# Parked blocks of the last weight matrix: stored split, loaded once, two quarters converted later

## The chip, the cores and the metric

The kernel runs on one core of a Trainium2 chip. The metric is the device time of one execution in microseconds (us), as the median of several runs. A core has a matrix engine (TensorE, PE in the profile, with its weight loads as PEld), a vector engine (VectorE, DVE), a scalar engine (ScalarE, ACT), GpSimd (POOL) and SyncE (SP). Here POOL and SP mostly issue DMA transfers. Each engine executes its own list of instructions in order; semaphores tie the lists to each other and to the transfers.

## The reference

Four stages follow each other over 2304 tokens (4 batches of 576) with 512 features:

```python
def phi(x):
    proj = einsum('bhsd,df->bhsf', x, w_phi)
    proj = proj - max(abs(proj), axis=-1, keepdims=True)
    return concatenate([exp(proj), exp(-proj)], axis=-1)
q_p, k_p = phi(q), phi(k)
kv = einsum('bhsf,bhsd->bhfd', k_p, v);  z = sum(k_p, axis=2)
x = einsum('bhsf,bhfd->bhsd', q_p, kv) / (einsum('bhsf,bhf->bhs', q_p, z) + 1e-6)
x = maximum(maximum(x @ w1, x @ w2), x @ w3) @ w_out      # 512 -> 768 -> 512
h = x @ w_in                                              # 512 -> 2048
out = (maximum(h, 0) + alpha * minimum(h, 0)) @ w_out2    # 2048 -> 512
```

Weights arrive as 64-bit floats, the rest as 32-bit floats.

## The kernel before, in words

**Arithmetic.** A float product is made of three PE products: each operand is split into a high part (`fp32r`, a rounded copy made on ACT at L70) and a low part (the difference, made on DVE at L76). `three()` lists high x high, high x low and low x high. A 64-bit weight is first converted by `from_f64` into a 32-bit word: one step on ACT (L83), four on DVE (L85, L87, L89, L91).

**Stages.** Linear attention fills the first part, interleaved with layer 1. Layer 1 (`layer1`, L427) makes three products in three PSUM banks `p1`, then the maximum: ACT copies the first (`s1`, L441), DVE takes the maximum with the second (L442) and the third (`ho`, L444), POOL stores it to h_d (L446). From about 324 us on only layer 1 is left (the tail, loop at L616); beside its products the weights of later layers are converted, `convert(2)` after each unit. Layer 2 (loop at L653, PE at L664) multiplies by w_out for eight chunks of 288 tokens, and stores sums and differences of the results (`yo`, `yt`) to y_d. Layer 3 (loop at L788, PE at L757) computes x @ w_in by seven products for each of 16 units (4 token tiles x 4 quarters of the features): `sums` in one double bank, copied by ACT as `s` (L766), with `pb` and `pc` in others; PReLU follows (L776, L777) and POOL stores `g` to g_d (L778). Layer 4 (loop at L823, PE at L841) makes the output in nine blocks of 256 tokens, two halves each; a half has seven factors `o` (`left`, L695: loads `a` from g_d, four sums or differences on DVE at L718 to L731, then seven splits) times seven blocks of the last weight matrix (`wq`), 84 matmuls a half.

**The last weight matrix.** It comes in four quarters p. For each, `do_quarters(p)` (L532) loads four pieces of 512 KB into "st" buffers (`big`, L499; three of them), converts them into words in "wt" buffers (`word`, L502; eight), and makes seven combined blocks with three differences and three more words (L517). `park` (L529) stores each block of 256 KB to q_d in DRAM; POOL issues the store (L530). The blocks are needed in layer 4 only, and until then no SBUF is free for them. `split_q` (L737), called in the last token tile of layer 3 and at the start of layer 4, fetches the 28 blocks: SP loads a word (L742), and ACT and DVE split it into a `wq` granule of 512 KB, in a slot (`ring`, `ring2`) that PE has released.

**Order.** `todo` is the list of conversion steps: quarters 0 to 3, w_out, then w_in (`do_quad`). `convert(n)` takes n steps from it and is called at fixed places. The framework's scheduler then sets the order of the instructions on each engine, by priorities and its own model of durations; the built program keeps that order. A buffer that is reused makes its next writer wait until all uses of the former content are done, the landing of a store included.

Of the kernel before, what the change touches and what calls it, by code (L numbers as in the profile page):

```python
# [10 lines left out]
F32 = mybir.dt.float32  # L11
F32R = mybir.dt.float32r
# [7 lines left out]
P = 128  # L20
# [33 lines left out]
def tile_kernel(ctx: ExitStack, tc: tile.TileContext, qT, kT, tails, v, w_phi, w1, w2, w3, w_out, w_in, w_out2, alpha, out):  # L54
# [11 lines left out]
    nc = tc.nc  # L66
# [36 lines left out]
    ring = ctx.enter_context(tc.tile_pool(name="ring", bufs=18, side="left"))  # L103
    dram = ctx.enter_context(tc.tile_pool(name="dram", bufs=1, space=DRAM))
# [4 lines left out]
    r_d = dram.tile([B, NPAIR, 2, S], F32, name="r_d")  # L109
    g_d = dram.tile([NF2, P, NTOK], F32, name="g_d")  # L110
    y_d = dram.tile([NT2, 7, P, 2 * CH], F32, name="y_d")
    q_d = dram.tile([4, 7, P, 512], F32, name="q_d")

    def bank(tag, bufs, nm):
        return ps.tile([P, 512], F32, tag=tag, bufs=bufs, name=nm)
# [342 lines left out]
    for i, pair in enumerate(pairs):  # L458
# [9 lines left out]
        for j in range(count):  # L468
            for _ in range(min(count, 4) if j == 0 else int(j + 3 < count)):
                fetch(begun[pair])  # L470
            with tc.high_priority(offset=LAST if i < NPAIR - 1 else 0):
                n = sum(len(x) for x in w)
                run(split_w123(n // 3, n % 3))
        u0 = 3 * (i - NPAIR) - LAG
        for u in range(u0, u0 + 3):
            if u >= 0:
                c, f = (u % 2, u // 2) if u < 12 else (u // NF1 % 2, u % NF1)
# [8 lines left out]
    def granule(pool, nm):  # L486

        return pool.tile([P, 2, 512], F32R, tag="w", name=nm)
# [8 lines left out]
            staged.append(st)  # L497

    def big(dtype, shape, nm):  # L499
        return sp.tile(shape, dtype, tag="st", bufs=3, name=nm)  # L500

    def word():  # L502
        return sp.tile([P, 512], F32, tag="wt", bufs=8, name="wt")
# [8 lines left out]
    def split(dst, src):  # L512
        hi_act(dst[:, 0], src)
        sub(V, dst[:, 1], src, dst[:, 0])
# [5 lines left out]
    wo, wi, wq = {}, {}, {}  # L520
# [5 lines left out]
    def do_out():  # L526
        return [lambda k=k: split_out(k) for k in range(NF1)], [w_out[k] for k in range(NF1)]

    def park(p, i, x):  # L529
        nc.gpsimd.dma_start(q_d[p, i], x)  # L530

    def do_quarters(p):  # L532
        b = {}

        def get(q):
            b[q] = words()

        def one():
            get(0)
            b[4] = both(word(), b[1], b[0])  # L540
            park(p, 0, b[0])
            park(p, 4, b[4])

        def two():
            get(3)
            park(p, 2, b[3])
            b[5] = both(word(), b[3], b[4])
            park(p, 5, b[5])
            park(p, 6, both(b[1], b[3], b[1]))

        def three_():
            get(2)
            park(p, 1, b[2])
            park(p, 3, both(word(), b[5], b[2]))

        return [lambda: get(1), one, two, three_], [w_out2[p, q] for q in (1, 0, 3, 2)]

    def do_quad(q):
        x = {}
        wi[q] = {}  # L560

        def get(n):
            x[n] = words()

        def to(i, n):
            pool = ring2 if (q == 0 and i < 4) or (q == 3 and i > 0) else ring
            wi[q][i] = granule(pool, "wi")
            split(wi[q][i], x[n])

        def second():  # L570
            get("22")
            x["s1"] = both(word(), x["21"], x["22"], ALU.add)

        def third():
            get("11")
            x["s2"] = both(word(), x["s1"], x["11"])
            x["s3"] = both(x["21"], x["11"], x["21"])
            to(0, "11")

        def fourth():  # L580
            get("12")
            to(1, "12")
            x["s4"] = both(x["12"], x["12"], x["s2"])

        steps = [lambda: get("21"), second, third, fourth]
        steps += [lambda i=i, n=n: to(i, n) for i, n in zip(range(2, 7), ("s2", "s1", "s3", "22", "s4"))]
        return steps, [w_in[q, a, b] for a, b in ((1, 0), (1, 1), (0, 0), (0, 1))]

    for steps, src in [do_quarters(p) for p in range(4)] + [do_out()] + [do_quad(q) for q in range(4)]:
        todo += steps  # L590
        sources += src

# [19 lines left out]
    def convert(n):  # L612
        for _ in range(min(n, len(todo))):
            todo.pop(0)()
# [38 lines left out]
    for c in range(2 * B):  # L653
        p2 = [double(tag, "p2") for tag in SETS[c % 2]]
        if c == 0:
            p2.reverse()
        if c + 1 < 2 * B:
            for kk in range(NF1 // 2):
                load_h(c + 1, kk)
        for ms in ((0, 1), (2, 3)) if c == 0 else (range(KT),):  # L660
            for k, m in ((k, m) for k in range(NF1) for m in ms):
                cs = slice(m * P, (m + 1) * P)
                for n, (x, y) in enumerate(three(wo[k][:, 0, cs], wo[k][:, 1, cs], *hs[c, k])):
                    nc.tensor.matmul(p2[m // 2][1][:, m % 2], x, y, start=k + n == 0, stop=k == NF1 - 1 and n == 2)  # L664
        tp = c // 2
        for b in range(2):
            Y[b, c % 2] = yo = z_tile("yo")
            A.activation(yo, p2[b][1], AF.Copy)
            if c % 2 == 0:
                nc.scalar.dma_start(y_d[tp, b], flat(yo))  # L670
        if c % 2:
            nc.scalar.dma_start(y_d[tp, 6], flat(Y[1, 1]))
            t1, t2, t3 = (z_tile("yt") for _ in range(3))
            both(t1, Y[0, 1], Y[0, 0])
            both(t2, Y[1, 1], t1)
            both(t3, Y[1, 1], Y[0, 1])
            t4 = both(Y[1, 0], Y[1, 0], t2)
            for i, t in zip((2, 3, 4, 5), (t2, t1, t3, t4)):
                nc.gpsimd.dma_start(y_d[tp, i], flat(t))
        if c == 2 * B - 1:  # L680
            for i in range(6):
                load_y(0, i)
        convert(3)

    T = P
    ORDER = (0, 5, 6, 4, 1, 3, 2)
# [50 lines left out]
    def split_q(count):  # L737
        for _ in range(count):
            n = len(wq)
            p, i = needs[n]  # L740
            wl = word()
            nc.sync.dma_start(wl, q_d[p, i])  # L742
            wq[p, i] = granule(ring if n < 16 or n >= 26 else ring2, "wq")
            split(wq[p, i], wl)

    load_y(0, 6)

# [40 lines left out]
    for n, (tp, q) in enumerate(units):  # L788
        sums, u1 = nxt
        if (tp, q) == (NT2 - 1, 0):  # L790
            convert(len(todo))
        g0, g1 = result(), result()
        _, pb = double("db", "pb")
        mults(pb, tp, q, 1, True)
        V.tensor_tensor(g0[:, :, 0], pb, u1, op=ALU.add)
        mults(sums, tp, q, 2, False)
        u2 = kept(sums)
        _, pc = double("dc", "pc")
        mults(pc, tp, q, 3, True)
        mults(sums, tp, q, 4, False)  # L800
        u3 = kept(sums)
        V.tensor_tensor(g1[:, :, 1], pc, u3, op=ALU.add)
        if n + 1 < len(units):
            nxt = begin(n + 1)
        mults(sums, tp, q, 5, False)
        A.activation(g1[:, :, 0], sums, AF.Copy)
        mults(pc, tp, q, 6, False)
        V.tensor_tensor(g0[:, :, 1], pc, u2, op=ALU.add)  # L808
        prelu(g1, tp, 4 * q + 2)
        prelu(g0, tp, 4 * q)  # L810
        convert(3)
        if tp == NT2 - 1:
            if q == 0:
                first = left(0, 0)
                run(first)
            split_q((2, 7, 7, 7)[q])
# [105 lines left out]
```

## Time and profile before

| | |
|---|---|
| median of 3 runs | 883.93 us (883.5 to 884.14) |
| profiled execution, its own time | 882.21 us |
| its span, first to last instruction | 880.4 us |
| PE busy | 869.1 us, 99% of the span |
| DVE, ACT, POOL busy | 678.7, 490.8, 158.3 us |
| bytes moved by DMA | 142.99 MB, mean 162 GB/s |
| mean granted TensorE clock | 0.998 of full speed |

The page of the profile gives busy times of the engines, the span in 40 slices, the DMA queues, the chain of work that ended last, and the groups of instructions with the idle time before them and what ended it. The trace behind it is read by views: the waits of an engine, the timeline of a window, busy times and DMA rates by window, and the time from issue to landing of transfers.

### The profile page before, as it was taken

To read this page: it belongs to the slowest core of one execution; us is meant where nothing else is said; L and a number is where in the kernel's file an instruction comes from. 1 tells how busy PE (TensorE), PEld (TensorE's weight loads), DVE (VectorE), ACT (ScalarE), POOL (GpSimd) and SP (SyncE) were. 2 spreads that over 40 slices of the span, in tenths; PEclk is the share of its full clock that TensorE was granted. 3 is DMA by queue.
4 is the path that set the end of the run, shared out by engine and by line. 5 is a ranking of instruction groups with operands and counts; after the bars stand their busy time and mean duration, and the time that the engine had idled before them with its cause. 6 is when DMAs were issued, how large, how long until landed. Compare 5 with 4: busy or idle time off the path is not lost.

```text
span 880.4 us, 17440 instructions
## 1 busy us (share of the span) xinstructions
PE 869.1 (99%) x6631; PEld 856.2 (97%) x6631; DVE 678.7 (77%) x1290; ACT 490.8 (56%) x1017; POOL 158.3 (18%) x278
## 2 busy tenths in 40 slices
PE   9999999999999999999999999999999999999998
PEld 8888999999999999999999999999999999999998
DVE  5689878778887879889999454746488889977791
ACT  4677657677776752334365354646477654444440
POOL 0354213222232135331101001111111100000000
PEclk9999999999999999999999999999999999999999
DMA  6455553222332158886489644835358645544321
GB/s 233 140 159 168 169 180 91 77 79 89 85 90 76 29 176 286 291 276 191 159 284 304 203 147 146 271 131 194 111 183 267 214 152 173 165 123 140 120 73 48
DMA packets 70436, 142.99 MB, mean 162 GB/s; under 512 B 9152, under 2 KB 36176, under 8 KB 70352
## 3 DMA queue, kind: packets, MB, share of 16 engines
q1 hardware_dynamic: 53664, 92.95, 33.8%
q0 software_dynamic: 14816, 45.26, 15.0%
q10 hardware_dynamic: 1872, 3.67, 1.2%
q8 instruction: 52, 0.85, 0.4%
q14 instruction: 32, 0.26, 0.1%
HBM read 93.07 MB, written 46.34 MB: 158 GB/s over the span
## 4 chain that ended last, share of the span: by engine, by line
PE 85%; DVE 6%; DMA 4%; issue 2%; ACT 1%; POOL 1%; DVEq 0%; POOLq 0%; ACTq 0%; SPq 0%
PE acc L841 20%; PE p L270 17%; PE sums L757 11%; PE p L664 8%; PE pj L270 6%; PE pn L270 6%; PE pc L757 6%; PE kvp L298 3%; PE kvp L311 3%; PE pb L757 3%; PE pt L373 2%; DVE wt L89 1%; DVE wt L91 1%; DMA xr<-h_d 1%; DMA nd<-nd 1%
## 5 line engine op out<-in xcount | busy, mean ns | idle before, releaser
L270 PE MATMUL p<-x,w123t 128*128 128x288 f32 x1728 | 249.1, 298 | 0.9 <-DVE ho L444 0.9
L270 PEld LDWEIGHTS p<-x,w123t 128*128 128x128 f32 x1728 | 234.5, 188 | 2.2 <-DVE ho L444 1.1
L841 PE MATMUL acc<-wq,o 128*128 128x256 f32 x1512 | 182.3, 283 | 2.5 <-ACT o L70 2.2
L841 PEld LDWEIGHTS acc<-wq,o 128*128 128x128 f32 x1512 | 181.5, 190 | 2.9 <-ACT o L70 2.4
L757 PE MATMUL sums<-x,wi 128*128 128x288 f32 x768 | 107.7, 295 | 0.3 <-ACT s L766 0.3
L757 PEld LDWEIGHTS sums<-x,wi 128*128 128x128 f32 x768 | 103.9, 188 | 0.6 <-ACT s L766 0.6
L664 PE MATMUL p<-x,wo 128*128 128x288 f32 x576 | 77.1, 296 | 1.5 <-ACT x L70 0.8
L664 PEld LDWEIGHTS p<-x,wo 128*128 128x128 f32 x576 | 76.6, 188 | 1.9 <-ACT x L70 1.0
L70 ACT ACTIVATE o<-wt 128x512 fp32r<-128x512 f32 x72 | 44.4, 629 | 56.4 <-PE acc L841 28.6
L777 DVE SCALAR_TENSOR_TENSOR g<-neg,al,g 128x576 f32<-128x576 f32 x64 | 50.1, 811 | 23.7 <-ACT neg L776 23.7
L217 DVE TENSOR_REDUCE mx<-pj 128x4 f32<-128x512 f32 (+1 forms) x80 | 49.7, 629 | 18.4 <-PE pj L270 18.1
L766 ACT ACTIVATE s<-sums 128x576 f32<-128x576 f32 x48 | 31.1, 648 | 45.4 <-PE sums L757 44.1
L778 POOL DMA_DIRECT2D g_d<-g x32 | 22.9, 714 | 162.5 <-DVE g L777 160.2
L446 POOL DMA_DIRECT2D h_d<-ho x48 | 27.8, 579 | 120.5 <-DVE ho L444 102.6
L76 DVE TENSOR_TENSOR o<-wt,o 128x512 fp32r<-128x512 f32 x72 | 48.0, 681 | 1.7 <-ACT o L70 1.7
L83 ACT ACTIVATE wt<-st 128x512 f32<-128x512 f32 x38 | 25.3, 673 | 41.7 <-DMA st<-in_w_out 33.4
L250 ACT ACTIVATE ke<-pj,mx 128x128 f32<-128x128 f32 x96 | 36.5, 380 | 20.1 <-DVE mx L217 20.1
L70 ACT ACTIVATE o<-a 128x512 fp32r<-128x512 f32 x54 | 33.1, 626 | 19.8 <-PE acc L841 18.5
L776 ACT ACTIVATE neg<-g 128x576 f32<-128x576 f32 x64 | 40.1, 675 | 6.2 <-DVE g L808 5.9
L251 ACT ACTIVATE ke<-pj,my 128x128 f32<-128x128 f32 x96 | 37.0, 386 | 11.0 <-DVE my L248 10.8
L298 PEld LDWEIGHTS kvp<-v,ke 128*128 128x128 f32 x320 | 40.1, 191 | 2.1 <-ACT ke L243 0.3
L298 PE MATMUL kvp<-v,ke 128*128 128x128 f32 x320 | 41.8, 276 | 0.0
(155 smaller groups left out, 1699.5 us busy)
## 6 DMA issues: line engine op xcount, KB each, us to landing
g_d<-g POOLq DMA_DIRECT2D x32, 576.0 KB, 3.6
a<-g_d SPq DMA_DIRECT2D x36, 512.0 KB, 4.4
st<-in_w_out SPq DMA_DIRECT2D x22, 512.0 KB, 5.3
wst<-in_w SPq DMA_DIRECT2D x18, 512.0 KB, 4.8
st<-in_w_in SPq DMA_DIRECT2D x16, 512.0 KB, 3.8
yr<-y_d SPq DMA_DIRECT2D x28, 288.0 KB, 3.4
v<-in_v SPq DMA_DIRECT2D x16, 480.0 KB, 3.6
q_d<-wt POOLq DMA_DIRECT2D x28, 256.0 KB, 6.0
```

The lines of the kernel that those rows point to most:

```text
L70: A.activation(dst, src, AF.Copy)
L76: eng.tensor_tensor(dst, src, hi.bitcast(F32), op=ALU.subtract)
L217: V.tensor_reduce(mx, pv, axis=AX.X, op=ALU.max, apply_absolute_value=True, negate=True)
L250: A.activation(ev[:, a, 0], pv[:, a], AF.Exp, bias=mx[:, a : a + 1])
L251: A.activation(ev[:, a, 1], pv[:, a], AF.Exp, bias=my[:, a : a + 1], scale=-1.0)
L270: nc.tensor.matmul(dst, x, y, start=i == 0, stop=i == len(ops) - 1, **kw)
L298: nc.tensor.matmul(kvp[:, j * P : (j + 1) * P], e[:, c], rv[:, t, j // 2 : j // 2 + 2].rearrange("p a d -> p (a d)"), start=first, stop=t ...
L664: nc.tensor.matmul(p2[m // 2][1][:, m % 2], x, y, start=k + n == 0, stop=k == NF1 - 1 and n == 2)
L757: nc.tensor.matmul(dst[:, j], a, b, start=start and n == 0, stop=n == len(ops) - 1, skip_group_check=True)
L776: A.activation(neg, gv[:, j], AF.Relu, scale=-1.0)
L777: V.scalar_tensor_tensor(gv[:, j], neg, al[:, f + j : f + j + 1], gv[:, j], op0=ALU.mult, op1=ALU.add)
L841: nc.tensor.matmul(acc[i], x, y, start=half == 0 and f == 0 and n == 0 and place[i][1] == 0, stop=half == 1 and f == 3 and n == 2, skip_gr ...
```

## The change

`park` no longer stores the word. It splits it into a tile "qt" of high and low part, taken from the "st" buffers (now four), and stores 512 KB. `split_q` loads these 512 KB straight into the granule; no word, no split. q_d is twice as large. Quarters 2 and 3 come last in the list of conversions, and fewer steps are taken in layer 2, so that they are converted late in layer 2 and in layer 3. A scratch area for DMA descriptors is halved, which gives room for the fourth buffer. Lines move by one to four (park's store is L532 then, `split_q`'s load L745).

```diff
-    q_d = dram.tile([4, 7, P, 512], F32, name="q_d")
+    q_d = dram.tile([4, 7, P, 1024], F32, name="q_d")
...
     def big(dtype, shape, nm):
-        return sp.tile(shape, dtype, tag="st", bufs=3, name=nm)
+        return sp.tile(shape, dtype, tag="st", bufs=4, name=nm)
...
     def park(p, i, x):
-        nc.gpsimd.dma_start(q_d[p, i], x)
+        t = big(F32R, [P, 2, 512], "qt")
+        split(t, x)
+        nc.gpsimd.dma_start(q_d[p, i], t.bitcast(F32).rearrange("p a n -> p (a n)"))
...
-    for steps, src in [do_quarters(p) for p in range(4)] + [do_out()] + [do_quad(q) for q in range(4)]:
+    order = [do_quarters(p) for p in range(2)] + [do_out()] + [do_quad(q) for q in range(4)]
+    for steps, src in order + [do_quarters(p) for p in range(2, 4)]:
...
-        convert(3)
+        convert((1, 2, 2, 3, 3, 3, 3, 3)[c])
...
-            wl = word()
-            nc.sync.dma_start(wl, q_d[p, i])
-            wq[p, i] = granule(ring if n < 16 or n >= 26 else ring2, "wq")
-            split(wq[p, i], wl)
+            wq[p, i] = t = granule(ring if n < 16 or n >= 26 else ring2, "wq")
+            nc.sync.dma_start(t.bitcast(F32).rearrange("p a n -> p (a n)"), q_d[p, i])
...
         prelu(g0, tp, 4 * q)
-        convert(3)
+        convert(1 if n else 3)
...
-    nc = bacc.Bacc("TRN2", target_bir_lowering=False, num_devices=1, dynamic_dma_scratch_size=8192)
+    nc = bacc.Bacc("TRN2", target_bir_lowering=False, num_devices=1, dynamic_dma_scratch_size=4096)
```

The instruction order of the two programs differs at many places; three matter below. The first is ACT in the layer-1 tail, between the copies `s1` of four successive units. What stands behind "waits" are the semaphores that an instruction waits for: DMASW are transfers issued by POOL, DMAHW those of SP and ACT. First the order before:

```order
L441 ACTIVATE s1_4120<-p1_4081 128x288 [waits DVE_49,PE_49]
L83 ACTIVATE wt_5233<-st_5117 128x512 [waits DMAHW2_49,DMASW1_49,DVE_49]
L441 ACTIVATE s1_4401<-p1_4362 128x288 [waits DVE_49,PE_49]
L83 ACTIVATE wt_5247<-st_5174 128x512 [waits DMAHW3_49,DMASW7_49]
L441 ACTIVATE s1_4446<-p1_4407 128x288 [waits DVE_49,PE_49]
```

and then the changed one:

```order
L441 ACTIVATE s1_4120<-p1_4081 128x288 [waits PE_49]
L70 ACTIVATE qt_5117<-wt_5115 128x512 [waits DMASW4_49]
L70 ACTIVATE qt_5122<-wt_5032 128x512 [waits DVE_49,Activation_49]
L441 ACTIVATE s1_4401<-p1_4362 128x288 [waits PE_49]
L70 ACTIVATE qt_5134<-wt_5126 128x512 [waits DMASW5_49,DVE_49,Activation_49]
L83 ACTIVATE wt_5260<-st_5132 128x512 [waits DMAHW2_49]
L70 ACTIVATE qt_5140<-wt_5138 128x512 [waits DMASW2_49,Activation_49]
L441 ACTIVATE s1_4446<-p1_4407 128x288 [waits PE_49]
```

The high copies of parked blocks (`qt`) now stand between the `s1` copies, three of the four shown waiting for an earlier store of POOL's, which held their slot.

The second is ACT from the end of layer 2 to the first `s` of layer 3 (`yo` is layer 2's result, `x` and `wi` operands of layer 3). Before:

```order
L668 ACTIVATE yo_6872<-p2_6798 128x576 [waits DMASW5_49,DMASW3_49,PE_49]
L70 ACTIVATE x_6918<-yr_6920 128x576 [waits DMAHW3_49,PE_49]
L668 ACTIVATE yo_6874<-p2_6799 128x576 [waits DMASW4_49,DMASW6_49,DVE_49,PE_49]
L70 ACTIVATE wi_7221<-wt_7086 128x512 [waits DVE_49]
L672 DMA y_d_69<-yo_6874 128x576 [waits Activation_49]
L766 ACTIVATE s_6971<-sums_6958 128x576 [waits DVE_49,PE_49]
```

Changed:

```order
L70 ACTIVATE wi_6924<-wt_6650 128x512 [waits PE_49]
L70 ACTIVATE qt_7339<-wt_7337 128x512 [waits DMASW1_49,DVE_49]
L83 ACTIVATE wt_7497<-st_7073 128x512
L70 ACTIVATE wi_7061<-wt_6756 128x512 [waits PE_49]
L671 ACTIVATE yo_6866<-p2_6792 128x576 [waits DMASW6_49,DMASW2_49,PE_49]
L70 ACTIVATE x_6912<-yr_6914 128x576 [waits DMAHW1_49,PE_49]
L671 ACTIVATE yo_6868<-p2_6793 128x576 [waits DMASW7_49,DMASW3_49,PE_49]
L70 ACTIVATE wi_7064<-wt_6780 128x512
L675 DMA y_d_69<-yo_6868 128x576 [waits Activation_49]
L70 ACTIVATE qt_7344<-wt_7067 128x512 [waits DMASW6_49,DVE_49]
L767 ACTIVATE s_6946<-sums_6933 128x576 [waits DVE_49,PE_49]
```

Two parks have come in, the second just ahead of `s`; it waits for the store of the first.

The third is DVE at the end of block 0 of layer 4. o_9225 to o_9247 are the factors of block 1's first half, a_9351 what is loaded for its second half, a_9218 a part of what the first half is made of. Before:

```order
L76 TENSOR_TENSOR o_9105<-wt_9082,o_9105 128x512 [waits Activation_49]
L76 TENSOR_TENSOR o_9225<-a_9217,o_9225 128x512 [waits DMAHW0_49,Activation_49]
L718 TENSOR_TENSOR wt_9221<-a_9217,a_9218 128x512 [waits DMAHW0_49]
L719 TENSOR_TENSOR wt_9222<-wt_9221,a_9217 128x512 [waits DVE_49]
L722 TENSOR_TENSOR wt_9223<-a_9217 128x512
L731 TENSOR_TENSOR wt_9224<-a_9218,wt_9222 128x512 [waits DVE_49]
```

Changed:

```order
L76 TENSOR_TENSOR o_9120<-wt_9097,o_9120 128x512
L721 TENSOR_TENSOR wt_9354<-a_9351 128x512
L76 TENSOR_TENSOR o_9230<-wt_9222,o_9230 128x512
L76 TENSOR_TENSOR o_9234<-wt_9223,o_9234 128x512
L76 TENSOR_TENSOR o_9237<-wt_9221,o_9237 128x512
L722 TENSOR_TENSOR wt_9355<-wt_9354,a_9351 128x512
L725 TENSOR_TENSOR wt_9356<-a_9351 128x512
L76 TENSOR_TENSOR o_9240<-a_9218,o_9240 128x512
L76 TENSOR_TENSOR o_9243<-a_9218,o_9243 128x512
L76 TENSOR_TENSOR o_9247<-wt_9224,o_9247 128x512
L76 TENSOR_TENSOR o_9225<-a_9217,o_9225 128x512
```

The low half of o_9225 has moved from behind the last factor of block 0 to the end of its group, and the first sum of a_9351 to the head of it.

## Rows read from the trace of the kernel before

**Rows 1.** Page, busy time of the engines
```profile
PE 869.1 (99%) x6631; PEld 856.2 (97%) x6631; DVE 678.7 (77%) x1290; ACT 490.8 (56%) x1017; POOL 158.3 (18%) x278
```
**Rows 2.** Waits of PE: what it waited for, us in total, times, longest
```profile
PE acc L841 <- ACT o L70: 2.2, 1, 2.2
...
PE p L270 <- DVE ho L444: 0.9, 1, 0.9
PE p L664 <- ACT x L70: 0.8, 1, 0.8
PE p L664 <- DVE x L76: 0.7, 1, 0.7
PE sums L757 <- ACT s L766: 0.3, 1, 0.3
```
**Rows 3.** Windows behind layer 4's stall: busy time by engine, PEclk, DMA share, GB/s
```profile
705.00:710.00 5.00, 4.52 (x23) 4.32 (x24) 4.90 (x9) 3.88 (x8) 0.00 (x0) 0.67 0.57 186
707.00:709.00 2.00, 2.00 (x11) 2.00 (x11) 2.00 (x5) 1.27 (x4) 0.00 (x0) 0.50 0.39 77
```
**Rows 4.** Landings of L530's stores; loads in 330 to 372; two windows of the tail
```profile
DMA to landing us min/median/max: 2.7/6.0/7.5
...
st<-in_w_out SPq DMA_DIRECT2D x10, 512.0 KB, 6.2
...
360.00:371.00 11.00, 10.64 (x81) 10.41 (x79) 9.16 (x20) 3.63 (x7) 3.43 (x7) 1.00 0.98 367
362.00:370.00 8.00, 8.00 (x63) 8.00 (x62) 6.19 (x15) 2.94 (x6) 2.64 (x5) 1.00 1.03 396
```
**Rows 5.** Layer-1 tail: timeline; groups by line (wq splits); chain (twelve matmuls)
```profile
334.30 1.12 POOL L530 DMA_DIRECT2D q_d<-wt  x2
...
369.60 0.39 ACT L441 ACTIVATE s<-p 128x288 f32<-128x288 f32 x1
...
L70 ACT ACTIVATE wq<-wt 128x512 fp32r<-128x512 f32 x28 | 17.4, 625 | 4.8 <-PE pc L757 1.9 <-DMA wt<-q_d 1.7 <-PE acc L841 1.1
...
L76 DVE TENSOR_TENSOR wq<-wt,wq 128x512 fp32r<-128x512 f32 x28 | 18.5, 685 | 6.7 <-ACT wq L70 6.7
...
694.59 1.61 PE sums L757 x12
```
**Rows 6.** Timeline at the start of layer 3: start us, us, engine
```profile
511.08 0.62 ACT L70 ACTIVATE wi<-wt 128x512 fp32r<-128x512 f32 x1
...
516.58 0.65 ACT L766 ACTIVATE s<-sums 128x576 f32<-128x576 f32 x1 [1.16 <-DVE yt L517]
...
511.88 0.68 DVE L76 TENSOR_TENSOR wi<-wt,wi 128x512 fp32r<-128x512 f32 x1
```
**Rows 7.** Median landings in 505 to 530 (y_d) and 650 to 715 (others)
```profile
y_d<-yt POOLq DMA_DIRECT2D x3, 288.0 KB, 3.7
...
g_d<-g POOLq DMA_DIRECT2D x10, 576.0 KB, 4.8
a<-g_d SPq DMA_DIRECT2D x5, 512.0 KB, 5.3
```
**Rows 8.** Timeline from the end of layer 3 to the end of layer 4
```profile
697.85 5.16 PE L841 MATMUL acc<-wq,o 128*128 128x256 f32 x42
...
700.18 1.29 DVE L76 TENSOR_TENSOR wq<-wt,wq 128x512 fp32r<-128x512 f32 x2
...
703.22 0.72 POOL L778 DMA_DIRECT2D g_d<-g  x1 [1.95 <-DVE g L777]
...
705.85 1.89 DVE L76 TENSOR_TENSOR o<-wt,o 128x512 fp32r<-128x512 f32 x3
...
706.89 0.37 SPq L705 DMA_DIRECT2D a<-g_d  x1
...
863.80 13.16 PE L841 MATMUL acc<-wq,o 128*128 128x256 f32 x110
```

## The prediction

> **What bounds the kernel now.** The page's busy times come first: TensorE (PE) is busy 869.1 of 880.4 us [rows 1], so all that a change can win is some 11 us of PE idle, and every wait that it adds on PE's path costs its full length. Next, PE's waits [rows 2]: after the start there are 0.9 us for a layer-1 maximum (`ho`), 0.8 + 0.7 us for the first `x` of layer 2, 0.3 us at the start of layer 3, and 2.2 + 0.3 us where layer 4 wants its second half's first operand `o`. That last stall also costs clock: in 705 to 710 us the granted clock was 0.67, with 0.50 (1.2 GHz) at 707 to 709 [rows 3]; 0.33 of 5 us is 1.7 us. The stall as a whole costs 2.2 + 0.3 + 1.7 = 4.2 us. It arises because ACT and DVE are still splitting `wq` words there and the `o` splits stand behind them. Third, the DMA rows [rows 4]: a 256-KB store to q_d took 6.0 us from issue to landing at the median, 2.7 at least and 7.5 at most; in the same stretch a 512-KB load took 6.2, and the most that both queues moved over 8 us was 396 GB/s, at a share of 1.03.
>
> **What moves.** Splits are neither added nor dropped: 28 on ACT and 28 on DVE leave the end of layer 3 and stand where the blocks are parked. Added are 28 x 256 KB to be stored and as many to be loaded, 14.7 MB. The other effect is on waiting. A word had its own ring of eight slots; a split block now lies in one of four "st" slots, shared with the weight loads, until its 512-KB store has landed. I go through four places on the clock of before.
>
> **1. Layer-1 tail, loss.** The 14 parks of quarters 0 and 1 stand on ACT between the `s1` copies that free PE's banks (first fence of the change). Six follow each other on one slot: qt_5054, 5117, 5140, 5211, 5274, 5297; each waits for the landing of the one before. The first store can be issued where before's two stores at 334.30 end, about 334.9 [rows 5]. A later step is a high copy of 0.63 us, a low one of 0.69 [rows 5], about 0.7 for one more DVE instruction ahead of it, and a landing. I take 6.2 us for the landing: it is the row of that size in that stretch. Then qt_5297's high copy can begin at 334.9 + 6.2 + 4 x 8.2 = 373.9 and ends at 374.5. Behind it stands the `s1` copy that ran at 369.60 before [rows 5]: 4.9 us late. On DVE a low copy, one conversion step and two shorter instructions stand ahead of the maximum that needs it, some 2.3 us. PE has 24 matmuls of layer 1, 3.2 us at 1.61 per 12 [rows 5], before it needs the bank. So PE stands 4.9 + 2.3 - 3.2 = 4.0 us in all; the 0.9 of [rows 2] is in the same place: **+3.1 us**. Five landings are in the chain, so 1 us more in each is 5 us: with the longest landing of 7.5 it is +9.6, and at 4.8 or less PE sees nothing, -0.9.
>
> The Trainium skill, page "DMA: Bandwidth & Descriptors", section "Anatomy of one DMA", gives a transfer as about 2.0 us and its bytes at 436 GB/s, so larger ones pay the fixed part once; 512 KB would be 3.2 us by it (an estimate from that page). By that rule this term would be -0.9. The trace does not agree for this stretch: half the bytes took 6.0 us.
>
> **2. Layer-1 tail, end, gain.** 14 parks with their conversions leave this stretch and a fourth slot lets loads run further ahead, so the first `x` of layer 2 should be on time: **-1.5 us** [rows 2]. If DVE stays the bound there, 0.
>
> **3. Start of layer 3, loss.** Quarter 2 is now converted late in layer 2. Its parks in the middle of layer 2 have ACT time to spare. But ACT has qt_7344 ahead of the first `s` of layer 3 (second fence of the change), and qt_7344 waits for the landing of qt_7339. Before, ACT's `wi` split at 511.08 and DVE's at 511.88 [rows 6] are the ones just ahead of qt_7339; ACT then makes its high half by 512.3, DVE its low half by 513.2, and POOL issues at 513.3. The landing is 3.7 us for 288 KB in this stretch, 4.8 for 576 KB in the end stretch [rows 7]; I take 4.8 as nearer in size: 518.1. Then qt_7344's copy (0.63) and `s` (0.65): 519.4, where `s` ended at 517.23 before [rows 6] and PE already waited: **+2.2 us**. With 3.7 it is +1.1, with 6.0 +3.4; not below +0.9, because DVE now has three more instructions ahead of the `yt` for which `s` also waits. Later parks of layer 3 stand behind products with time to spare.
>
> **4. End of layer 3 and blocks 0 and 1 of layer 4.** The 4.2 us go as they are: ACT and DVE have no `wq` split left, and DVE's two at 700.18 are gone from between the last products [rows 8], so the last store of `g`, issued at 703.22 before, goes at about 701.9. What is late next is the loads of `g` for block 1's second half, a_9351. In the changed order DVE takes the sum of a_9351 before the low halves that block 1's first half needs (third fence of the change): o_9225, which PE wants first, is the tenth instruction from there. When does a_9351 land? It is queued on SP behind the 28 `wq` loads, each of which waits until PE has released its slot. PE releases the first of those slots 336 matmuls, about 43.7 us, before the last one, near 659.3, and the last at 703.0, where PE's row of 42 ends [rows 8]. From 659.3 on the queues have to move 28 x 0.524 MB of `wq`, 8 stores of `g` at 0.590 and three `a` at 0.524, together 21.0 MB. At 396 GB/s [rows 4] that takes 53.0 us: 712.3, and I put the landing at 713. Ten DVE instructions at 0.63 (three took 1.89 [rows 8]) are 6.3: 719.3. PE's need: it ended at 876.96, and eight blocks are 1344 matmuls at 0.1196 (13.16 for 110 [rows 8]), which gives 716.2 for block 1; less the 4.2 that are gone, 712.0, and 1.4 for the 12 matmuls before the low half is used, 713.4. PE stands 5.9 us, and I add the same 1.7 for the clock: 7.6 in place of 4.2, **+3.4 us**. Bounds: without any backlog the loads go at 705.6 (3.67 after the store, as from 703.22 to 706.89 [rows 8]) and land 5.3 [rows 7] to 5.6 us later, at 711.2: 4.1 us, and -0.1 if the clock holds. At the 367 GB/s of 360 to 371 us [rows 4] it is 717.4, so 12.0 us and +7.8.
>
> The same page of the Trainium skill, section "Specifications", puts a core's share of the memory at some 358 GB/s, which speaks against storing and loading twice the bytes. With it the 21.0 MB would end near 718 (an estimate from that page). The 396 GB/s of the trace are above it, so I keep the row.
>
> **Sum.** 3.1 - 1.5 + 2.2 + 3.4 = +7.2 us on the profiled execution's 882.21, 889.4. That execution is 1.7 below the median of the runs, 883.93; on the median the forecast is **891.1 us**. A difference of 0.2%, 1.8 us, is about what a measurement of this kernel can tell from none.
>
> **Rivals.**
> *A, faster, the other side: transfers are quick.* If the last `g` store lands after 2.7 us and a_9351 after another 2.7, as the quickest q_d store did [rows 4], it lands near 707.3 and DVE reaches o_9225 at 713.6, where PE wants it at 713.4: 707 is the point that decides, and each us later costs one. With landings under 4.8 the front is hidden too: -0.9 - 1.5 + 0.9 - 4.2 = -5.7, 878.2. For it: the splits do leave a place where PE demonstrably waited. Against it: the median landings, and the SP queue. The fit of the skill's DMA page leads here. Chance 0.16.
> *B, it cancels.* Front hidden, start of layer 3 at its least, end at its bound without backlog: -0.9 - 1.5 + 0.9 - 0.1 = -1.6, 882.3. Chance 0.11.
> *C, the front alone is hidden* (landings under 4.8 there): -0.9 - 1.5 + 2.2 + 3.4 = +3.2, 887.1. For it: quarters 2 and 3 no longer follow in this stretch. Chance 0.14.
> *D, DMA-bound.* Landings of 7 us in the front (+7.1), 367 GB/s at the end (+7.8): 7.1 - 1.5 + 2.2 + 7.8 = +15.6, 899.5. For it: the share was already about 1 there and bytes per block double. Chance 0.12.
> That the change doesn't do what it says is excluded by the order: no `wq` split is left in it.
>
> **How the numbers follow.** The forecast has 0.47, its own range 888 to 896. Faster is A, 0.16; the same is B, 0.11; slower is C, D and the forecast, 0.73. From 881.5 to 899 about 0.8 is held: most of A and half of D lie outside.
>
> **What would show it.** Front: ACT waits at the `qt` copies ended by q_d stores, and PE waits for `ho` of 3 to 5 us in all between 340 and 380. Layer 3: one PE wait for `s` of about 2.5 us. End: no wait at 703, a wait of PE for a low half `o` of 4 to 8 us near 713, a lower clock behind it, and DVE idle for a_9351 just before. The forecast is wrong if q_d stores land in under 4.8 us in the tail, or if a_9351 lands before 708.

## The result, and the profile after

The changed kernel takes 890.7 us at the median of six runs (889.76 to 891.99), the kernel before beside it 883.85 (six runs, 882.34 to 886.05): ratio 1.0077, 95% interval [1.0061, 1.0092]. It is slower by 6.9 us. The profiled execution took 891.34 us with a span of 889.6 and a mean granted clock of 0.994; before 882.21, 880.4 and 0.998.

Total and sign are as forecast, the terms of the sum are not. Cutting each profiled execution at the first matmul of layer 2, the first of layer 3's `sums` and the first `acc` of layer 4 gives, in us:

| stretch | before | after | difference | forecast |
|---|---|---|---|---|
| start to layer 2 | 435.17 | 437.38 | +2.2 | +3.1 |
| layer 2 | 78.44 | 76.45 | -2.0 | -1.5 |
| layer 3 | 172.90 | 174.11 | +1.2 | +2.2 |
| layer 4 to the end of PE | 190.45 | 198.13 | +7.7 | +3.4 |

The differences add up to 9.1 us, not to the 6.9 of the medians: the profiled execution of before was 1.6 us quicker than the median, that of after 0.6 slower. Of the first +2.2, 1.9 are there before the layer-1 tail begins: the group of attention's `pn` products out of `qh` that starts at 320.08 before starts at 321.97 after, with the same order on PE up to there. In every execution profiled below this point came later than in that one execution of before, by 1.1 to 3.9 us. So the tail itself lost some 0.3 us.

Page of the kernel after, busy time (beside [rows 1]):

```profile
PE 872.9 (98%) x6631; PEld 858.6 (97%) x6631; DVE 679.9 (76%) x1290; ACT 489.7 (55%) x1017; POOL 159.4 (18%) x278
```

Waits of PE after (us in total, times, longest), to be laid beside [rows 2]:

```profile
PE acc L842 <- DVE o L76: 7.0, 3, 3.5
...
PE sums L758 <- ACT s L767: 1.3, 2, 1.0
...
PE acc L842 <- DMA wq<-q_d: 0.7, 2, 0.3
PE p L270 <- ACT s L441: 0.6, 1, 0.6
```

The two waits of layer 2 are gone, the tail's wait is 0.6 where it was 0.9, and the large one is DVE's low half `o` in layer 4. The timeline of PE (start us, us; in brackets the idle time just before) says where:

```profile
375.24 62.30 PE L270 MATMUL p<-x,w123t 128*128 128x288 f32 x468 [0.64 <-ACT s L441]
518.14 1.86 PE L758 MATMUL sums<-x,wi 128*128 128x288 f32 x12 [0.97 <-ACT s L767]
...
706.03 8.53 PE L842 MATMUL acc<-wq,o 128*128 128x256 f32 x70 [1.35 <-DVE o L76]
714.88 0.94 PE L842 MATMUL acc<-wq,o 128*128 128x256 f32 x6 [0.32 <-DMA wq<-q_d]
716.16 1.45 PE L842 MATMUL acc<-wq,o 128*128 128x256 f32 x10 [0.34 <-DMA wq<-q_d]
721.08 2.07 PE L842 MATMUL acc<-wq,o 128*128 128x256 f32 x8 [3.46 <-DVE o L76]
725.29 160.78 PE L842 MATMUL acc<-wq,o 128*128 128x256 f32 x1332 [2.15 <-DVE o L76]
```

The ten matmuls at 716.16 are the last six of block 0, which wait for the last `wq` block, and the first four of block 1. PE stands from 717.6 on: until 721.08 for the low half of o_9234, then, after eight matmuls, until 725.29 for that of o_9225. After it the clock is at half speed. Windows (bounds, length, then busy time of PE, PEld, DVE, ACT, POOL, then PEclk, DMA share, GB/s):

```profile
720.00:722.00 2.00, 0.93 (x4) 0.93 (x5) 2.00 (x4) 0.00 (x0) 0.00 (x0) 0.61 0.00 0
722.00:724.00 2.00, 1.15 (x6) 0.85 (x4) 2.00 (x5) 1.66 (x3) 0.00 (x0) 0.50 0.04 8
724.00:726.00 2.00, 0.71 (x3) 0.71 (x4) 2.00 (x5) 1.92 (x5) 0.00 (x0) 0.50 0.28 50
726.00:728.00 2.00, 2.00 (x11) 2.00 (x11) 2.00 (x4) 0.63 (x1) 0.00 (x0) 0.50 0.61 212
728.00:730.00 2.00, 2.00 (x12) 2.00 (x11) 2.00 (x5) 0.00 (x0) 0.00 (x0) 0.50 0.40 89
730.00:732.00 2.00, 2.00 (x16) 2.00 (x16) 2.00 (x5) 0.00 (x0) 0.00 (x0) 0.83 0.72 205
```

Busy time times the missing share of the clock, 0.93 x 0.39 + (1.15 + 0.71 + 4.00) x 0.50 + 2.00 x 0.17, is 3.6 us of work lost besides the waits. From 722 to 730 it is the lower level, 1.2 GHz, after PE had been idle from 717.6 to 721.08; the second stall lies inside that stretch.

DVE's timeline shows what it stood at (the rows left out are the ones between):

```profile
708.90 0.69 DVE L76 TENSOR_TENSOR o<-wt,o 128x512 fp32r<-128x512 f32 x1
719.12 0.69 DVE L721 TENSOR_TENSOR wt<-a 128x512 f32<-128x512 f32 x1 [9.54 <-DMA a<-g_d]
719.73 1.89 DVE L76 TENSOR_TENSOR o<-wt,o 128x512 fp32r<-128x512 f32 x3
...
724.55 1.29 DVE L76 TENSOR_TENSOR o<-a,o 128x512 fp32r<-128x512 f32 x2
```

DVE was idle for 9.5 us, waiting for a_9351, with block 1's first low halves queued behind that sum, as the third fence of the change's order has them. o_9225 is the first of the two at 724.55. The chain that ended last (start, us, what) says why the load was late:

```profile
701.56 0.72 POOL g_d L779
...
703.13 8.78 DMA g_d<-g
...
712.11 0.37 SPq L708
...
712.53 6.52 DMA a<-g_d
```

The last store of `g` needs 8.78 us, only then can SP issue the load that reads it, and that takes 6.52. Before, SP issued it 3.67 us behind the store's issue [rows 8]; here 8.98, from 703.13 to 712.11, of which SP stood 7.1 us for the store's landing alone. Windows and landings (median us, 650 to 715) show the reason: the queues are full until the store has landed, and a `wq` load takes 9.8 us.

```profile
680.00:700.00 20.00, 20.00 (x158) 20.00 (x158) 6.81 (x10) 7.70 (x12) 1.44 (x2) 1.00 1.03 412
700.00:704.00 4.00, 4.00 (x36) 4.00 (x35) 3.94 (x6) 3.43 (x7) 1.43 (x2) 1.00 1.03 403
704.00:708.00 4.00, 2.65 (x22) 2.44 (x21) 4.00 (x8) 4.00 (x9) 0.00 (x0) 1.00 1.03 418
708.00:712.00 4.00, 4.00 (x36) 4.00 (x35) 1.58 (x3) 1.12 (x3) 0.00 (x0) 1.00 1.02 417
```
```profile
wq<-q_d SPq DMA_DIRECT2D x28, 512.0 KB, 9.8
g_d<-g POOLq DMA_DIRECT2D x10, 576.0 KB, 7.8
a<-g_d SPq DMA_DIRECT2D x5, 512.0 KB, 6.5
```

### The profile page after: what moved, and what is told of

Read it like the earlier page. It is cut to its first block, busy times and chain, and to the rows that moved or that the text cites. A ratio compares the mean times of both kernels' runs of the same rounds, so it can differ in the third digit from the quotient of the medians.

```text
span 889.6 us, 17349 instructions
## 1 busy us (share of the span) xinstructions
PE 872.9 (98%) x6631; PEld 858.6 (97%) x6631; DVE 679.9 (76%) x1290; ACT 489.7 (55%) x1017; POOL 159.4 (18%) x278
## 3 DMA queue, kind: packets, MB, share of 16 engines
q0 software_dynamic: 16608, 52.60, 16.9%
q10 hardware_dynamic: 1872, 3.67, 1.2%
## 4 chain that ended last, share of the span: by engine, by line
PE 68%; issue 17%; DVE 5%; DMA 5%; POOL 4%; ACT 1%; POOLq 0%; SPq 0%; DVEq 0%; ACTq 0%
PE acc L842 18%; PE p L270 13%; PE sums L758 10%; PE pj L270 6%; PE pn L270 5%; PE pc L758 5%; PE kvp L298 3%; PE kvp L311 3%; PE pb L758 2%; PE pt L373 2%; DMA q_d<-qt 1%; POOL q_d L532 1%; DMA g_d<-g 1%; POOL y_d L682 1%; DMA r_d<-dc 1%
## 5 line engine op out<-in xcount | busy, mean ns | idle before, releaser
L842 PE MATMUL acc<-wq,o 128*128 128x256 f32 x1512 | 184.6, 285 | 7.6 <-DVE o L76 7.0
L251 ACT ACTIVATE ke<-pj,my 128x128 f32<-128x128 f32 x96 | 37.1, 387 | 11.2 <-DVE my L248 11.0
L405 POOL DMA_DIRECT2D xr<-r_d x64 | 34.5, 545 | 37.0 <-DMA r_d<-dc 25.8
```

Of the source, the lines that this page charges most:

```text
L251: A.activation(ev[:, a, 1], pv[:, a], AF.Exp, bias=my[:, a : a + 1], scale=-1.0)
L842: nc.tensor.matmul(acc[i], x, y, start=half == 0 and f == 0 and n == 0 and place[i][1] == 0, stop=half == 1 and f == 3 and n == 2, skip_gr ...
```

## The experiments

The theory: layer 4 loses because two things meet, the load of a_9351 that is late by the bytes queued ahead of it, and DVE's order, which has that load's first sum ahead of block 1's low halves. The rivals: the order alone; the bytes alone, with PE waiting for the `wq` or `a` data themselves; the moved conversions; the scratch area for descriptors. Stretches below are cut as in the table above, each out of one profiled execution.

**e1: the sum held back.** In the changed kernel the first sum of block 1's second half is recorded behind the first and the third low half of its first half; nothing else.

```diff
-            sub(V, ov[:, 1], src, ov[:, 0])
+            lows[block, half, i] = V.tensor_tensor(ov[:, 1], src, ov[:, 0].bitcast(F32), op=ALU.subtract).ins
...
-        V.tensor_tensor(s1, a10, a11, op=ALU.add)
+        if (block, half) == (1, 1):
+            with tc.issue_after(lows[1, 0, 0]), tc.issue_after(lows[1, 0, 2]):
+                V.tensor_tensor(s1, a10, a11, op=ALU.add)
+        else:
+            V.tensor_tensor(s1, a10, a11, op=ALU.add)
```

> The changed kernel with one DVE instruction held back: the first sum of a_9351 may only come after the low halves of block 1's first half (o_9225 to o_9247). Transfers stay as they are. If the order of DVE is what turned the late load into a PE stall, the waits of 3.5 and 2.2 us near 721 to 725 and the low clock behind them (some 3.6 us of work) go: 881.5 to 884 us, with 1.4 + 0.7 us of waits left. Rival: the doubled bytes bound this stretch by themselves; then PE waits as long for a wq load or for the second half's operands, and the time stays above 888.

Measured: 881.3 us (879.39 to 883.13), before beside it 884.68; ratio 0.9952 [0.9937, 0.9968]. Layer 4 takes 188.39 us in place of 198.13. DVE and PE of e1:

```profile
718.97 0.69 DVE L725 TENSOR_TENSOR wt<-a 128x512 f32<-128x512 f32 x1 [5.00 <-DMA a<-g_d]
```
```profile
706.20 9.48 PE L848 MATMUL acc<-wq,o 128*128 128x256 f32 x76 [1.35 <-DVE o L719]
715.95 160.56 PE L848 MATMUL acc<-wq,o 128*128 128x256 f32 x1350 [0.27 <-DMA wq<-q_d]
```

The load is as late as in the changed kernel (DVE starts the sum at 718.97, there at 719.12), DVE still stands 5.0 us for it, and PE does not stand in block 1 at all: the low halves are done. So lateness alone costs nothing there; "the bytes alone" is out. This version is faster than both kernels, than the one before by 3.4 us.

**e2: words again.** The changed kernel with words of 256 KB parked, loaded and split as before; the fourth buffer, the order of conversion and the scratch stay changed.

```diff
-        t = big(F32R, [P, 2, 512], "qt")
-        split(t, x)
-        nc.gpsimd.dma_start(q_d[p, i], t.bitcast(F32).rearrange("p a n -> p (a n)"))
+        nc.gpsimd.dma_start(q_d[p, i], x)
```

> The changed kernel with the parks and reloads as before (256-KB words, split on ACT and DVE at the end), but with four st buffers, the late quarters 2 and 3 and fewer conversions in layer 2. If the doubled bytes are the cause of the end's loss, it goes to that of before (4.2 us) or less and the gain of 2 us at the start of layer 2 stays: 881 to 884 us. Rival: the DVE order, in which the sum of a_9351 stands ahead of o_9225 here too, costs by itself; a_9351 then lands near 711 to 712 and PE waits 2 to 4 us near 717: 885 to 888 us. If converting late in layer 3 costs, layer 3 shows waits that before has not.

Measured: 889.75 us (886.69 to 891.48), 1.0046 [1.0026, 1.0066], above what either side gave. Layer 4 is 193.35, without the stall in block 1, but layer 2 takes 79.21 and layer 3 177.43: PE waits 2.9 us for the first `s`, which stands behind DVE's `yt` (ACT idle 2.50 for it). The run speaks for the bytes as one condition of layer 4's loss. From e3, below, it differs only in when quarters 2 and 3 are converted: with words, converting them late costs 6.7 us. Layer 2's wait for the first `x` is back here (1.96 us) although the fourth buffer is in.

**e3: only the fourth buffer**, in the kernel before (the smaller scratch makes room for it).

```diff
-        return sp.tile(shape, dtype, tag="st", bufs=3, name=nm)
+        return sp.tile(shape, dtype, tag="st", bufs=4, name=nm)
...
-dynamic_dma_scratch_size=8192)
+dynamic_dma_scratch_size=4096)
```

> The kernel before with only the fourth st buffer and the smaller scratch. If the gain at the start of layer 2 comes from loads running further ahead, PE's 1.5 us of waits there go: 882 us, less what the end loses by the DVE order that comes with it (a_9351 ahead of o_9225), 0 to 3 us: 882 to 885. Rival: the gain came from the conversions that were moved away; then the waits of 0.8 and 0.7 us stay, and 884 to 887.

Measured: 883.03 us, 0.9992 [0.9974, 1.001]. Layer 2 falls from 78.44 to 76.46, as in the changed kernel: the fourth buffer is enough for term 2's gain. And DVE's order at block 1 is already that of the changed kernel, a_9351's sum first and o_9225 last, yet there is no stall there: the load is nearly on time. DVE of e3:

```profile
its engine sat idle before it (us, times) until:
  DMA a<-g_d: 1.0, 1
```

Layer 4 is 192.28, its two waits (2.2 and 2.1 us) standing where the splits are:

```profile
706.34 170.97 PE L841 MATMUL acc<-wq,o 128*128 128x256 f32 x1426 [2.11 <-DVE o L76]
```

So the order alone costs no stall in block 1, and it was the fourth buffer that brought it. It is not free, though: the same order has the four sums of block 1's first half, from a_9218, ahead of block 0's low halves, and this second wait, 0.3 us before, stands behind them. Layer 4 is 1.8 us longer than before.

**e4: three buffers in the changed kernel** (`bufs=4` back to `bufs=3`).

> The changed kernel with three st buffers in place of four. The store chain of the layer-1 tail tightens: if the landing of stores limits the tail at all, PE waits there of 3 to 8 us in place of 0.6. DVE's order at block 1 is that of before again (o_9225 early), so of the end's loss 4 to 6 us go if the order is its cause. Together 886 to 894; what tells is the split: tail wait up, end wait down. Rival: the bytes are the end's cause; then the end waits stay at 6 to 8 us in all, and 893 to 898.

Measured: 898.43 us, 1.015 [1.0125, 1.0175]; three buffers cost 7.7 us more (6.9 against the kernel before, measured beside each). Layer 4 takes 196.87. Its waits of PE:

```profile
PE acc L842 <- ACT o L70: 4.7, 1, 4.7
PE sums L758 <- ACT s L767: 3.7, 2, 2.6
...
PE p L270 <- DVE s L442: 1.4, 2, 1.2
PE p L270 <- DVE ho L444: 1.0, 1, 1.0
```

PE waits 2.4 us in the tail, less than expected (e7, with four slots, has as much), and 3.7 at layer 3. For layer 4 the expectation failed: the waits stay at 6.6 us in all, which is what the rival, the bytes, had named. The reason can be read from DVE:

```profile
729.86 0.69 DVE L721 TENSOR_TENSOR wt<-a 128x512 f32<-128x512 f32 x1 [12.25 <-DMA a<-g_d]
```

In layer 4 DVE's order is that of before there, with o_9225 ahead of all sums of block 1, and PE stands all the same: behind o_9225 comes the sum of a_9217 and a_9218, both operands of block 1's first half, whose load is now the late one (DVE idle 12.25 us for it; the last store of `g` took 8.44, the load 7.00). They lie in the same ring of buffers as the parks. So an early o_9225 is no cure where the operands themselves are late.

**e5: only the smaller scratch**, in the kernel before (the last two lines of e3's diff).

> The kernel before with only the smaller scratch for descriptors. All kernels with the small scratch reached 82 us of the profile 1.6 to 3.4 us later than the kernel before, with the same order of instructions up to there. If the scratch is the cause, this one does too: 885 to 887 us. Rival: it is chance or the placement of buffers; then it comes there at the same time as before, and 883 to 885.

Measured: 884.81 us beside 884.79, 1.001 [0.9988, 1.0032]: no effect that can be told. Its attention, too, came out longer than in the profiled execution of before, by 2.0 us at 82 us and 3.0 at 320, the sign that was expected if the scratch were the cause, while the median is the rival's. This execution took 886.70, 1.9 above the kernel's own median. How much of the table's first row is the execution's and how much the scratch's stays open; by the interval the scratch can cost 2.8 us at most. Its layer 2 took 80.85 us, 2.4 more than before with the same code there.

**e6: a second hold.** e1, and block 1's first sum behind the first low half of block 0's second half.

```diff
+        elif (block, half) == (1, 0):
+            with tc.issue_after(lows[0, 1, 0]):
+                V.tensor_tensor(s1, a10, a11, op=ALU.add)
```

> e1 with a second instruction held back: the first sum for block 1's first half (from a_9218) may only come after the low half of o_9098, the first factor of block 0's second half. The wait of 1.3 us near 706 goes if that sum's late data are its cause: 0.5 to 1.5 us below e1, 880 to 881. Rival: PE then waits for the wq loads that are late by about as much, and the time stays.

Measured: 882.45 us, 0.9975 [0.9956, 0.9994]. PE's 1.35 us for `o` at 706 are gone and it runs into this:

```profile
PE acc L851 <- DMA wq<-q_d: 2.9, 1, 2.9
```

What was won for `o` is lost a few matmuls later, and more, to a `wq` block that was issued at 699.86 and took 11.50 us: layer 4 takes 190.55, in e1 188.39. The queues moved 403 to 421 GB/s meanwhile, which fits a limit by the bytes once the order is right; no run with both holds and fewer bytes shows it.

**e7: e1 with a scratch of 6144** in place of 4096.

> e1 with a scratch of 6144 in place of 4096. If the small scratch costs 1.7 us near 62 to 82 us, part or all of it comes back: 879.5 to 881. Rival: no effect of the scratch, as e1: 881 to 882.

Measured: 882.49 us, 0.9975 [0.9954, 0.9995], layer 4 187.82. No gain over e1; between these two sizes of the scratch no effect can be told in layer 4 either.

**e8: e3 with e1's hold**: words, four buffers, the sum held back.

> The kernel before with four st buffers, the small scratch and the same hold on the sum of a_9351, words and splits as before. It tells what the split parks are worth by themselves. If the splits at the end are the bound there, the waits of 2.2 and 2.1 us near 703 stay and the time is that of e3, 882 to 884, above e1. Rival: the order was all, and this comes to 880 to 881, as e1 or below.

Measured: 883.09 us, 0.9981 [0.9959, 1.0003], layer 4 193.41. The hold gives nothing without the late load. Layer 4 in us:

| | order of the changed kernel | sum held back |
|---|---|---|
| words (e3, e8) | 192.28 | 193.41 |
| split blocks (after, e1) | 198.13 | 188.39 |

Split blocks lose 5.9 us with the one order and win 5.0 with the other. The later runs repeat the cells within 0.9 us: e9 197.94 and e10 187.56 with split blocks, e11 192.28 and e12 193.19 with half of them as words.

**e9: all quarters converted first, as before**; the rest of the change stays.

```diff
-    order = [do_quarters(p) for p in range(2)] + [do_out()] + [do_quad(q) for q in range(4)]
-    for steps, src in order + [do_quarters(p) for p in range(2, 4)]:
+    for steps, src in [do_quarters(p) for p in range(4)] + [do_out()] + [do_quad(q) for q in range(4)]:
...
-        convert((1, 2, 2, 3, 3, 3, 3, 3)[c])
+        convert(3)
...
-        convert(1 if n else 3)
+        convert(3)
```

> Split parks and four slots, but all four quarters converted first and three steps a chunk, as before: only the moved conversions are undone. Theory (the end is lost by DVE's order and the late load of a_9351, the moved conversions cost only the wait for s at the start of layer 3): the end stretch stays as in the changed kernel, 197 to 199 us from the first acc to the end, with a PE wait for o of 2 us or more near 721; layer 3 goes back to 173 us. In the layer-1 tail 28 parks follow each other on the slots instead of 14, 14 landings of 4.8 us more on the chain, so PE waits 3 to 8 us there. In all 889 to 896. Rival (the moved conversions make the end late): 188 to 192 us in the end stretch, in all below 886.

Measured: 900.01 us (899.37 to 900.63), 1.0174 [1.0144, 1.0205]; more than expected. Layer 4 is 197.94, as forecast: the moved conversions have no part in its loss. PE:

```profile
PE acc L841 <- DVE o L76: 8.3, 3, 3.5
PE p L666 <- DVE ho L444: 3.0, 1, 3.0
PE sums L757 <- ACT s L766: 2.6, 2, 1.6
...
PE p L666 <- ACT x L70: 1.6, 1, 1.6
```

That 28 parks in the tail would cost is as expected (ACT is idle 16.9 us for their stores), though PE pays it mostly behind the tail, 4.6 us at layer 2, where DVE's last maximum (`ho`) and ACT's `x` come late. But layer 3 did not go back to 173 us; it took 175.48, with a longer wait for `s`. The expectation that this wait belongs to the moved conversions fell. Here `s` stands behind DVE's `yt` (ACT idle 2.98 us for it), and DVE still converts: it is busy 19.86 of 20 us from 440 to 460 and 17.8 to 18.9 in each 20 us from there to 520. That the lateness is handed on from the tail is argued, not shown.

**e10: e9 with e1's hold.**

> The same with block 1's sum of a_9351 held behind the first and third low half of its first half. Theory: the end stretch falls by 8 to 10 us against the run without the hold, to 188 to 190; in all 880 to 887, which is above or at the changed kernel with the hold if the 14 further parks are not hidden in the tail. Rival (they are hidden there): 878 to 881, the fastest of all, since layer 3's wait is gone too.

Measured: 890.84 us, 1.0065 [1.0043, 1.0086], 9.2 us below e9; layer 4 187.56. The hold is worth the same here. The total is above what was expected. It is 9.5 us above e1, as e9 is 9.3 above the changed kernel (9.1 and 8.1 against the kernel before, measured beside each): so much converting two quarters late is worth once blocks are parked split, where with words it cost 6.7 (e2 against e3).

**e11: half the quarters as words.** Blocks of quarters 0 and 1 split, of 2 and 3 as words, conversion as before. The last 14 loads of blocks have half the bytes, and 14 splits are back on ACT and DVE; else it is e9.

```diff
+        if p not in (0, 1):
+            nc.gpsimd.dma_start(q_d[p, i, :, :512], x)
+            return
         t = big(F32R, [P, 2, 512], "qt")
```

> Blocks of quarters 0 and 1 are parked split, those of quarters 2 and 3 as words, in the order of conversion of before: the last 14 loads ahead of block 0 have half the bytes, 3.7 MB less, and 14 splits stand again on ACT and DVE. DVE takes a_9351's sum just as early as in the changed kernel. Theory (the load of a_9351 is late because the last store of g and the load stand behind the queued bytes): 3.7 MB at some 410 GB/s are 9 us, so a_9351 lands near 711 on the clock of before and the wait for o behind it near 721 is gone; what is left are 2 to 4 us where the splits stand ahead of o. The end stretch 190 to 194 us, in all 882 to 887. Rival (the order alone does it): the end stretch at 197 or more.

Measured: 888.1 us (885.45 to 891.08), 1.0038 [1.002, 1.0055], about a us above what was expected. Layer 4 is 192.28. DVE's order is that of the changed kernel, and DVE waits 1.0 us for the load in place of 9.5:

```profile
717.28 0.69 DVE L723 TENSOR_TENSOR wt<-a 128x512 f32<-128x512 f32 x1 [1.00 <-DMA a<-g_d]
```
```profile
704.00:708.00 4.00, 3.85 (x33) 3.64 (x31) 4.00 (x7) 2.73 (x5) 0.96 (x2) 1.00 0.51 108
```

The queues moved 108 GB/s in the same 4 us in which they moved 418 after. So with the order left alone the landing follows what is queued. The other profiles agree: SP issues the next load of `g` 3.5 to 4.2 us behind the last store's issue in the seven kernels whose last loads are words (before, e2, e3, e5, e8, e11, e12), and 8.6 to 9.2 in the seven with split blocks. The stall behind it is gone, and two waits of 2.3 and 2.1 us at the splits are back.

**e12: e11 with e1's hold.**

> The same with the hold. Theory: with a_9351 landing early the hold has nothing to win, end stretch within 1.5 us of the run without it. Rival (order alone): 188 to 190, 7 or more below it.

Measured: 888.95 us, 1.0038 [1.0017, 1.0059], layer 4 193.19, 0.9 from e11: with the load on time the hold has nothing to win, as in e8.

## Why the prediction was right, and where its steps were wrong

**The total** fell on the forecast by luck, because errors cancelled: the front was put 2.8 us too high, layer 2 0.5 and layer 3 1.0, layer 4 4.3 too low. That is the count with attention's 1.9 us left out; the profiled execution itself was forecast at 889.4 and took 891.34.

**Term 1, +3.1, was +0.3.** The chain came near the time forecast, by a path that is partly another. ACT of the kernel after:

```profile
365.92 0.63 ACT L70 ACTIVATE qt<-wt 128x512 fp32r<-128x512 f32 x1 [1.00 <-DMA q_d<-qt]
...
372.56 0.66 ACT L83 ACTIVATE wt<-st 128x512 f32<-128x512 f32 x1 [4.34 <-DMA st<-in_w_out]
...
374.26 0.63 ACT L70 ACTIVATE qt<-wt 128x512 fp32r<-128x512 f32 x1
374.80 0.69 ACT L441 ACTIVATE s<-p 128x288 f32<-128x288 f32 x2
```

The `qt` copies did wait for stores, but only 4.2 us in four waits from 320 to 380; qt_5297, at 374.26, did not. ACT had stood 4.34 us for a weight load, and that load had been issued late, at 368.22, because SP waited 4.3 us for a q_d store to free its slot. The stores landed in 5.6 us at the median from 330 to 380, where 6.2 were taken. qt_5297's copy was forecast for 373.9; with the 1.9 us that this execution was late by then it would be 375.8. The `s1` copy behind it was forecast 4.9 us late and started at 374.80 in place of 369.60, less the 1.9: 3.3. "PE has 24 matmuls of layer 1, 3.2 us, before it needs the bank" held: the matmul that waits at 375.24 for [0.64 <-ACT s L441] is the first on that bank in the built program, 24 behind the product that the copy reads. What failed is the lateness, 3.3 in place of 4.9, and above all the step that adds 2.3 us of DVE there. The copy alone frees this bank; the maximum frees the unit's second one, and PE wants that 24 matmuls later still, since by then units take turns between two sets of three banks (`spread`, L430). DVE reached that maximum at 376.53, PE the bank some 3.2 us after 375.24. So 3.3 and the copy's own 0.4 less the 3.2 are some 0.5 us; 0.64 was seen, in place of 4.0.

**Term 2, -1.5, was -2.0.** In the kernel before the fourth buffer is enough for it (e3, e8). It is not enough everywhere: e2, e9 and e11 have it too, take 79.21, 79.87 and 80.78, and wait for `x` again. What holds `x` up there stays open.

**Term 3, +2.2, was +1.2.** Place and mechanism are right:

```profile
513.69 0.54 POOL L532 DMA_DIRECT2D q_d<-qt  x1 [14.59 <-DVE qt L76]
...
516.79 0.63 ACT L70 ACTIVATE qt<-wt 128x512 fp32r<-128x512 f32 x1 [1.10 <-DMA q_d<-qt]
517.44 0.65 ACT L767 ACTIVATE s<-sums 128x576 f32<-128x576 f32 x1
```

ACT has qt_7344 ahead of `s` and waits for a store. Mis-sized was that landing: POOL issued it at 513.69 and ACT went on at 516.79, 3.1 us where 4.8 were taken; the bound named for 3.7 was +1.1. The row nearest in time (288 KB, 3.7) would have been the better choice than the one nearest in size.

**Term 4, +3.4, was +7.7.** DVE's order, the late a_9351 and PE's wait for low halves, 4 to 8 us, all came, the wait at 717.6 in place of 713.4 and in two parts, the first for o_9234 and only the second for o_9225. Three sizes were off. First, the landing: forecast 713, which is 714.4 on the clock of after (layer 4 begins 1.4 later), seen 719.0. "The queues have to move 21.0 MB" was right in bytes and in rate (403 to 418 GB/s until 712), but it treated the load as one more transfer in the stream. It can be issued only once the last `g` store has landed, and that store waits its turn among the `wq` loads: 8.78 us, and then 6.52. Bytes at a rate give the end of a queue; two dependent transfers behind it are a chain. Second, "the 4.2 us go as they are": 1.35 us of `o` at 706 stayed, behind the sums of a_9218 (e6), and 0.66 for `wq` came new. These moved PE's need to 717.6, so that the stall itself grew only from 5.9 to 7.7, in which PE worked for 2.07 at half clock. Third, the clock: 3.6 us of work lost, where the 1.7 of the old stall were taken; the longer stall was followed by a longer stretch at 0.50. Together 5.6 + 2.0 + 3.6 = 11.2 in place of 7.6. That explains 3.6 of the 4.3. The rest is mostly the old stall, which was priced too high: e1's layer 4 ran at a mean clock of 1.000 and less its waits of 1.35 and 0.27 took 186.8, so that, by an estimate from these single executions, before lost 3.7 in place of 4.2 and after 11.4.

**The rivals.** A had the right condition, that a_9351's landing decides. It did not happen by a faster landing; e1 reached its end by taking the order away. C (the front hidden, the rest as forecast, 887.1) is what the front did. D's rate of 367 GB/s was not seen: it was 403 to 418.

## What to carry to other kernels

Where an operand is loaded from what was just stored, price store and load as a chain behind whatever is queued, not by bytes at a rate; and look at what stands behind its first use on that engine. An order that costs nothing at a place while a load is on time can cost several us when it is late: hold the first use behind work that is ready, then test both together, since neither the order nor the bytes show the loss alone. Before pricing a late release on the engine that bounds, find out which instruction frees which buffer, and count the work up to its next use: here the copy and the maximum free two different banks, and PE wants them 24 matmuls apart.

## What the runs showed of the hardware

A store of 576 KB issued by POOL, 4.8 us from issue to landing before [rows 7], took 8.78, 8.44 and 8.52 us (after, e4, e9) while SP's `wq` loads were queued, although it goes by another queue. The Trainium skill, page "DMA: Bandwidth & Descriptors", section "Queues, rings and completion order", says that an engine takes turns between its queues, a packet each. By that, an estimate from that page for packets of one size, the two last stores (1.18 MB) would have half of 417 GB/s and need some 5.7 us; the trace has 10.4, from 701.55 to 711.91, with 28.0% of the DMA engines' time for POOL's queue and 73.9% for SP's from 701.6 to 711.9. That agrees with a shared engine, not with an even share.

The queues moved 403 to 418 GB/s, stores and loads together, for 32 us (680 to 712). The 358 of the same page's "Specifications", weighed in the prediction, did not bind here.

What a stall costs was not its length alone: after the stall of 3.46 us, with the one of 2.15 us in between, PE had eight us at 0.50, 3.6 us of work with the edges. In e1 the 1.35 us at 706 were followed by no lower clock: 1.00 from 700 to 720, and a mean of 1.000.
